# A written-out instruction order for local attention and a two-layer network: its first quarter ordered anew

## Chip, cores and metric

One core of one Trainium2 chip. The metric is the device time of one execution in microseconds (us), the median of the runs. In the text, PE is TensorE, DVE is VectorE, ACT is ScalarE, POOL is GpSimd and SP is SyncE, as the profile names them.

## What is computed

Attention with a window and a few global keys, then a two-layer network with a squared ReLU:

```python
# q, k, v: (4, 8, 768, 64) = batch, heads, sequence, head_dim; n_global 8, n_local 96
scores = scale * np.matmul(q, k.transpose(0, 1, 3, 2))
rel = pos[:, None] - pos[None, :]
is_global = pos[None, :] < n_global
is_local = (rel >= 0) & (rel < n_local)
dist = np.where(is_global & ~is_local, n_local, np.abs(rel))
scores = np.where(is_global | is_local, scores - slopes[:, None, None] * dist, -1e9)
a = softmax(scores)
x = (a @ v).transpose(0, 2, 1, 3).reshape(3072, 512)
h = np.maximum(x @ w_in, 0.0)      # w_in: 512 x 2048
return (h * h) @ w_out             # w_out: 2048 x 512
```

Inputs and output are float32; the kernel works in 16-bit floats with 32-bit sums.

## The kernel before

The 3072 tokens are cut into tiles of 128. Three tiles make a half, two halves a batch; there are eight halves, 0 to 7. Because of the window, a tile of queries needs the keys of its own tile ("own") and of the tile before ("before"); the global keys stand in the first 32 rows of a copy of the tile before (`kb` for keys, `vb` for values; "key fix" and "value copy" below).

For the first two halves (one batch) the work is listed job by job in `OPENING`. Its names are used throughout, with r for the tile, 0 to 5:

- T0, T1: TensorE transposes of q and k of tiles 0 and 1 (`turn_first`, L1233); Qr, Kr the same for a later tile (`turn_tile`, L1279).
- Pro, Prb: the distance term of the scores of tile r, own or before (`distances`, L1300). Sro, Srb: the scores (`score_tile`, L1314). ACT takes their exponent; for r from 3 on DVE multiplies by a mask (L1359).
- Ari: weights times values for two of the four head pairs, i = 0 or 1 (`attend_tile`, L1368); DVE normalises the result (L1392, L1394: "norm"). Xri: transposes of the normalised tile into `xt`, the input of layer 1 (`tile_to_x`, L1400).
- F, G, D, E: layer 1 (`layer1`, L705). Fc is four blocks of 128 hidden units for tile 0; Gci two blocks for tiles 1 and 2; Ec i and Dc the same for half 1. Later blocks of half 1 are single, with 384 columns.

From half 2 on, attention runs by head pair (`turn`, `score`, `attend`), and the two layers use sums of blocks, with seven products in place of eight. Those sums are DVE work.

The four weight loads of `w_in` (c0 to c3), the four of `w_out`, and all loads of q, k, v tiles except the first two tiles of q and k go through GpSimd's queue (L396, L454, L461). The queue is in order: a load that waits holds all behind it. The tiles `sq` and `sk` that loads of q and k write are one buffer each from half 2 on, so a load for half 3 waits until half 2's turns have read them. Half 1's q and k are staged in the memory that later holds `w_mix`, hence that name in the profile.

Nothing is scheduled while the program is built. `ORDER` is a list of words, and `Plan.run` calls the operations in that order; each engine executes its own in the order in which they were called and waits only for its data. A word is an engine's letter and a number: p is the n-th TensorE job in order of listing, l the n-th load, and a, d, g, s the n-th other operation, given to ACT, DVE, POOL or SP. What stands behind a dot names the PSUM banks (there are eight) that the job takes; behind a plus, the time to fill with idle matmuls; behind an @, an operation that the load follows. So the table fixes three things: the order on each engine, the engine of an operation that ACT or DVE could do, and the banks. A bank is free for the next job when the operation that reads it out has run.

Of the kernel before, what the change touches and what calls it, by code (L numbers as in the profile page):

```python
# [9 lines left out]
FP16 = mybir.dt.float16  # L10
# [3 lines left out]
P = 128  # L14
# [37 lines left out]
ORDER = """a4 d1 g2 p0.0 a6 s8 d12 a0 s10 d13 l3 l1 a18 l2 d15 d19 a26 d16 d3 l5 a30 d14 a20 a27 d9 l4 a23  # L52
d5 a22 d17 p1.12+31 a21 l0 p5.34 d11 a7 p10.56 l6 a28 p3 a24 l10 a31 d32 l9 a33 p6 d34 p4.7 a39
l7 p11 d37 a29 p9.0 p8.1 a46 l8 p2.23 d43 a40 p19.7 d35 l11 a47 p7 d55 a25 p13.51 d36 l13 a41
d44 p14.4 p12.67 d48 p15 a42 l12 d59 p17 a49 p16.0 p22.2 d45 l14 p24.4 a52 d51 p23.36 a50 d38
p34.50 l16 d58 a53 p21.7 d64 p25.2 a60 l18 p27.1 d65 a57 p20.4 a61 p32.37 d66 a81 d56 p31.2 l15
a73 p29.6 d68 p18.5 d72 p28.4 a74 p26.3 l19 p36.1 d54 a69 p35.2 p30.7 a86 d70 p33.54 d85 a71 d91
p39.16 a67 p40.27 a77 d63 p37.3 a82 d75 l17 a78 d62 p41.5 a92 d79 d76 p38.0 d84 d80 p45.4 d83
l21 a97 p48.1 d96 a101 l20 a98 p44.2 a89 p47.5 d107 l23 p46.7 a112 p42.0 d111 a108 d110 a93
p43.2 d109 p53.1 a87 p52.5 d102 p50.4 p49.7 a113 l22 d120 d100 a90 d105 p59.6 l27 a116 d119 a103  # L60
d106 p55.3 p51.1 l29 d94 a122 a88 d128 p65.2 l28 a104 d95 a117 p64.4 a118 p58.5 a129 a136 d114
p60.0 d99 a137 l30 d146 d191 p54.3 l24 p62.6 d115 d205 l25 p57.1 a133 p56.4 d125 d121 p63.7
p67.6 a123 d134 d135 a130 d206 p61.1 p72.3 a126 d132 p69.4 d189 a124 p77.7 a131 d156 p70.0 a142
p82.1 d157 d165 a159 p71.5 a160 p74.4 d162 l34 a166 d201 a163 p83.6 d147 a161 l26 p73.0 a167
d522 d164 a138 p84.3 l31 d158 d148 a168 a169 p79.52 d186 l35 a139 d202 p89.04 p81.1 d127 a198
l33 d151 p85 a187 d170 a178 d523 p86 a174 d207 a199 d184 p78.06 a179 d149 l32 p80.57 p88.41 d180
p87 a195 l36 d200 a175 p76.2 d203 a185 l37 d155 p75.4 a196 d193 p91.0 l38 a188 d143 s194 d197
p66.1 a181 l39 d172 a171 p95.3 d152 a173 p90.5 d223 p100.4 d153 a209 s224 a176 d236 p92 d204
p103.2 d177 d208 p68.3 d237 s216 a244 a140 d210 p93.6 d240 a211 p94 a182 d150 s217 a144 d219
p96.1 p104 d225 p97 d183 a245 d221 p98.7 s220 d239 a218 p102.3 d238 p111 d214 d228 s226 l44 p106  # L70
d222 d243 l43 d213 p109.61 s229 d227 p110.73 d154 p99 l40@217 a255 d258 s215 d141 p101 a256
l42@217 d145 a251 d272 d190 p113 l45 a252 a234 p114.73 d254 l41@217 d192 p108.61 p105.0 a248 l46
d246 a261 p107 d253 d259 a262 l47 d257 s260 p115.62 a249 s235 d230 p116.74 l48 p118.3 a264 d250
p131.1 a265 d232 d263 p117.6 a268 d231 a292 p122.2 d266 a273 p121.7 d233 a269 d212 p125.1 a271
d280 s324 p124 d284 p127.4 a283 p126 d241 a278 d267 p123.6 d285 a293 p137.1 s325 d281 p119.5
a287 p132 a286 p129.7 a279 d294 p130 p140 d323 a301 p142 d270 p134.6 a290 d274 a307 p128.1 a291
p135 d288 p133.2 a308 p136 d298 p141.5 a310 d300 s242 a299 p143.1 s282 a297 d309 p139 d326 p138
d524 p112 d395 l50@325 a305 s275 d311 p120 a303 l56 d306 a312 s289 d295 a302 p146.36 l53 p147.54
d304 p145.71 a330 s296 d313 l51@325 a333 p144.2 a331 d318 l52 p148.3 a334 d319 a276 l49@325
p149.5 d321 a327 a322 d433 d332 a328 l54 p151.64 p150.07 d314 p152 d320 a338 l57 d329 p159.1  # L80
a339 l55 p157.0 d336 a337 p172.7 a341 d340 p153 a352 d370 a342 p160.3 a350 d315 p169.6 s371 d353
a344 p158.7 p162 d351 p161 p154.4 d316 a355 d397 p166.3 a347 p164.7 d356 p163 s398 p156 d317
d358 d359 a366 p171.1 d343 p165 s399 p167 a360 d362 p181.7 a363 d335 a361 p170 d345 p175 d367
p177 a357 p174.0 d375 p173.5 a378 d373 p178.3 s247 s277 d369 p176 a383 s354 p180 d368 a372
p155.0 d349 a379 p168.1 a376 d382 a384 d400 p179 p183 l58@399 a364 p182.7 d380 a348 p184 s374
a377 l65 d385 p185.3 a389 l62 a387 d381 s386 p188.41 a365 d388 p187.05 l59@399 p186.27 a405
p189.6 d401 a409 l63 a413 d402 p190.0 a406 d416 l73 a410 d403 p191 a407 l61 d396 a414 p193.42
d412 a417 p194.65 l60@399 d411 a418 p192.71 p195 a422 d415 a419 l64 d391 p200.4 d429 a420 p206.7
d437 a426 p198.0 d392 p219.1 s438 d393 a434 d408 a427 p207.6 p204.4 d394 a447 s346 d489 p210
d443 a462 p202.5 a451 d428 p199.1 a423 d404 p211 a441 p213 d435 p197.4 p217.2 a432 d456 p205.5  # L90
s436 p218.1 d424 a444 d452 p196 d480 s491 a445 d476 a461 d460 p203.6 p215.7 d442 p223 a458 p221
d425 a453 p208 d421 s492 p209 d481 p220 a448 d483 p222.1 a469 d477 p214 a446 d467 p227.6 s390
d431 s468 p212.0 d457 p201 d449 a464 d493 a463 p216.1 d454 p224 a484 l70 p225 d459 s455 p230
a439 d473 a471 l66 d465 p226 a496 p231.50 d470 a474 l69@492 s430 p236.13 d478 p233.42 a497 s490
p228.7 d472 a503 l72 d482 a498 p229.5 l67@492 a509 d479 d494 a504 p241.4 l71 p235 a510 d485 d475
a527 d505 p237.01 a495 l68@492 a466 p232.72 d499 p234 l74 a500 d525 d486 a450 p245.3 d506 l75
p240.7 d508 p247 a512 s507 d515 p246.5 a533 p239 d488 a532 d487 d516 a526 p255 a501 p250 d520
p259.0 d544 s521 p249.2 d531 p243.6 d536 p252 a535 p238.3 d529 a540 d517 a513 p253 a549 d502
p261.5 s576 a519 p256 d514 p257.6 p270 d545 p263 d546 p244 a551 s440 a553 d541 a565 p248.1 d511
a530 p268.6 p272 d561 p267 a534 p251.2 d560 p260.4 a566 s562 p262 d537 p269 d550 p258.6 a542  # L100
p266 s547 d548 p242.4 a563 d538 a568 p254.0 a552 s577 d518 p264 a528 p271 a578 d554 p274 d567
d543 p265.7 p273 d579 p275 a580 a555 d569 p279 d558 a564 p281.2 d556 a596 a570 p276.60 a559 d585
s557 d571 p277.54 p278.71 a586 p280 d600 a593 s539 a589 d601 p282.6 a604 d603 a587 p286 a594
d598 d602 a590 p284.75 a605 d588 p283.03 p285.14 a609 p289 d595 a616 a613 s599 d668 p291 s574
a606 d619 d581 a607 p288.7 d572 p290.1 d622 a610 s575 d582 p303.0 a620 d591 p306.3 a639 d612
s573 p294 d608 a618 a643 d611 p323.5 a614 d671 d626 p305.4 p307 d642 p310 a644 p292.6 d584 d621
p295 a623 p321.4 d583 a628 d647 p296 d664 p312 d615 p298 s665 a629 p301 d650 p287.1 d632 p308.3
a617 s627 p297.4 d636 s597 p322 d645 p313.2 a666 d592 p299.6 a651 d631 p314 a648 p293.0 d652
p311.4 d624 p300 p316 d649 p315 a635 s625 p318.0 a633 d669 p302.4 d672 p309 a634 d655 p320 a667
p304 d653 p326 a662 d637 p324.2 d658 s638 a679 p325.7 a663 d646 s659 d640 p317 a678 p319 p335.4  # L110
# [94 lines left out]
def kernel(  # L205
# [11 lines left out]
    nc = tc.nc  # L217
# [1270 lines left out]
    for op in [*slope_ops, *mask_ops, *first]:  # L1488
        op.follows = [table_op]
# [117 lines left out]
```

## Time and profile before

| | us |
|---|---|
| median of 3 runs (lowest, highest) | 200.62 (200.59, 200.8) |
| the profiled execution | 200.43 |
| its span, first to last instruction | 198.7 |
| TensorE busy in the span | 191.6 |
| VectorE busy | 176.3 |
| ScalarE busy | 151.0 |
| GpSimd busy (nearly all of it issues loads) | 66.9 |

Rows of a view of groups or of the timeline give the start, the busy time, the engine, the line of the kernel and the operation with the tile that it writes and those that it reads. In square brackets is the idle time of the engine just before and what ended it. Rows of the waits give the total, the number and the longest. A load's row gives its size and the time from issue to landing.

### The profile page before, as it was taken

How to read it: one execution, taken by the hardware profiler on the slowest of the kernel's cores; microseconds unless marked ns; L12 is line 12 of the kernel's file. 1: busy time of each engine (PE TensorE's matmuls, PEld its weight loads, DVE VectorE, ACT ScalarE, POOL GpSimd, SP SyncE). 2: the span in 40 equal slices, each digit the busy share in tenths (PEclk: the TensorE clock that was granted, in tenths of full speed). 3: DMA queues.
4: the chain of work that ended last, by engine and by line, in shares of the span. 5: the costliest groups of instructions: out<-in, count | busy, mean ns of one | idle time of the engine just before them, and what ended most of it. 6: DMA issues, size and time to landing. Idle time of an engine off the chain costs nothing.

```text
span 198.7 us, 5980 instructions
## 1 busy us (share of the span) xinstructions
PE 191.6 (96%) x2381; PEld 163.2 (82%) x2381; DVE 176.3 (89%) x450; ACT 151.0 (76%) x321; POOL 66.9 (34%) x82
## 2 busy tenths in 40 slices
PE   7798999999999999999999999999999999999993
PEld 3576899856888687788888998999889999999993
DVE  7589696899999999999989999899899996978971
ACT  6799797899555888976999679878897578769211
POOL 8996565187108701940194007800000000000000
PEclk9999999999999999999999999999999999999999
DMA  5999999999999998999899799996531221201214
GB/s 152 182 150 194 189 180 172 209 195 155 182 192 92 155 205 218 107 127 145 218 118 153 104 222 129 161 175 147 102 102 37 94 57 40 109 0 53 109 53 158
DMA packets 106987, 27.52 MB, mean 139 GB/s; under 512 B 97104, under 2 KB 104016, under 8 KB 106960
## 3 DMA queue, kind: packets, MB, share of 16 engines
q0 software_dynamic: 74944, 13.11, 90.1%
q1 hardware_dynamic: 30816, 13.45, 31.7%
q10 hardware_dynamic: 1200, 0.59, 1.1%
q8 instruction: 18, 0.29, 0.6%
q14 instruction: 9, 0.07, 0.1%
HBM read 27.26 MB, written 6.29 MB: 169 GB/s over the span
## 4 chain that ended last, share of the span: by engine, by line
PE 78%; DMA 7%; POOL 5%; DVE 5%; ACT 3%; issue 1%; POOLq 0%; DVEq 0%
PE yps L1064 32%; PE hps L841 19%; PE hps L717 14%; PE sp L610 4%; DMA xt<-tm 4%; DMA w_mix<-in_k_dram 4%; PE av L671 3%; PE yps L978 3%; POOL w_mix L396 2%; POOL v L396 1%; DVE hr L901 1%; ACT h L758 1%; PE av L1380 1%; PE trp L549 1%; DVE vb L258 1%
## 5 line engine op out<-in xcount | busy, mean ns | idle before, releaser
L623 ACT ACTIVATE ex<-sp 128x512 f16<-128x512 f32 x66 | 36.7, 632 | 3.6 <-PE sp L610 3.5
L1064 PEld LDWEIGHTS <-h 128*128 128x128 f16 x376 | 33.9, 98 | 4.0
L717 PE MATMUL hps<-xt,w_in_sb 128*128 128x128 f16 (+2 forms) x288 | 35.6, 273 | 0.3 <-ACT ex L1350 0.3
L256 ACT COPY kept<-hps 128x384 f32<-128x384 f32 x52 | 24.6, 490 | 12.4 <-PE hps L841 8.8
L901 DVE CUSTOM_DVE_ANT_0 hr<-hps,kept 128x384 f16<-128x384 f32 x58 | 30.3, 548 | 1.0 <-PE hps L841 0.6
L717 PEld LDWEIGHTS <-w_in_sb 128*128 128x128 f16 x288 | 23.5, 98 | 5.9 <-DMA w_in_sb<-in_moe_w_in_dram 0.5
L1064 PEld LDWEIGHTS <-mixed 128*128 128x128 f16 x272 | 25.2, 98 | 3.6 <-DVE mixed L1029 0.2
L396 POOL DMA_DIRECT2D sq<-in_q_dram x19 | 17.3, 910 | 31.0 <-DMA q<-sq 23.4
L256 ACT COPY y<-yps 128x256 f32<-128x256 f32 (+2 forms) x39 | 14.6, 385 | 15.8 <-PE yps L1064 15.8
L396 POOL DMA_DIRECT2D sk<-in_k_dram x19 | 17.1, 903 | 24.9 <-DMA q<-sq 22.4
L841 PEld LDWEIGHTS <-w_in_sb 128*128 128x128 f16 x288 | 24.4, 98 | 1.0
L841 PEld LDWEIGHTS <-in_mix 128*128 128x128 f16 x272 | 22.8, 98 | 1.1 <-issue 0.3
L841 PE MATMUL hps<-x_mix,in_mix 128*128 128x192 f16 x204 | 23.4, 246 | 0.0
L1064 PE MATMUL yps<-w_mix,h 128*128 128x256 f16 (+1 forms) x192 | 22.4, 264 | 0.0
L1064 PE MATMUL yps<-w_mix,mixed 128*128 128x256 f16 (+1 forms) x184 | 22.2, 268 | 0.0
L396 POOL DMA_DIRECT2D v<-in_v_dram x24 | 21.8, 922 | 1.2 <-DVE h L760 0.6
L1064 PE MATMUL yps<-w_out_sb,h 128*128 128x256 f16 (+1 forms) x184 | 21.9, 268 | 0.0
L924 ACT ACTIVATE h<-hr 128x768 f16<-128x768 f16 x25 | 20.9, 857 | 0.0
L647 DVE TENSOR_TENSOR phat<-ex,mask 128x1024 f16<-128x1024 f16 (+1 forms) x36 | 20.6, 590 | 0.1
L744 ACT ACTIVATE hr<-hps 128x384 f16<-128x384 f32 (+1 forms) x35 | 18.5, 546 | 2.8 <-PE hps L717 2.8
L841 PE MATMUL hps<-xt,w_in_sb 128*128 128x192 f16 x172 | 19.8, 246 | 0.0
L1126 DVE TENSOR_TENSOR y<-yps,y 128x256 f32<-128x256 f32 (+1 forms) x30 | 11.9, 408 | 3.5 <-PE yps L1064 2.9
(110 smaller groups left out, 354.1 us busy)
## 6 DMA issues: line engine op xcount, KB each, us to landing
out_dram<-y SPq DMA_DIRECT2D x23, 256.0 KB, 2.6
v<-in_v_dram POOLq DMA_DIRECT2D x24, 128.0 KB, 7.1
sq<-in_q_dram POOLq DMA_DIRECT2D x19, 128.0 KB, 6.4
sk<-in_k_dram POOLq DMA_DIRECT2D x19, 128.0 KB, 6.4
w_in_sb<-in_moe_w_in_dram POOLq DMA_DIRECT2D x4, 512.0 KB, 11.0
w_out_sb<-in_moe_w_out_dram POOLq DMA_DIRECT2D x4, 512.0 KB, 12.3
y<-in_q_dram SPq DMA_DIRECT2D x2, 256.0 KB, 4.4
y<-in_k_dram ACTq DMA_DIRECT2D x2, 256.0 KB, 5.1
```

The source lines that it names most:

```text
L256: nc.scalar.copy(out=out, in_=in_)
L396: dma = nc.gpsimd.dma_start(out=dst, in_=src[x.b, :, r0 + t * P:r0 + (t + 1) * P, :] .rearrange("h p d -> p h d"))
L610: nc.tensor.matmul(sp[h][:, i, :], lhsT=lhsT, rhs=x.q[rows, r % HT, a, :], start=True, stop=True)
L623: nc.scalar.activation(out=st["ex"][:, h], in_=sp[h], func=AF.Exp, scale=scale)
L647: eng(e).tensor_tensor(out=x.phat[a][:, :, t0:t0 + n], op=ALU.mult, in0=st["ex"][:, :, i0:i0 + 2 * n].rearrange("p e (t b) c -> p e t (b c ...
L717: nc.tensor.matmul(st["ps"][:, i * n:(i + 1) * n], lhsT=w_in_sb[:, kk, m * P:(m + 1) * P], rhs=x.xt[:, kk, c0:c1], start=kk == 0, stop=kk ...
L744: nc.scalar.activation(out=o, in_=i, func=AF.Relu)
L841: nc.tensor.matmul(st[name][:, i * HC:(i + 1) * HC], lhsT=left(i, kk), rhs=right(kk), start=fresh and i == kk == 0, stop=kk == KK - 1, ski ...
L901: eng(e)._custom_dve(dve_ops.TENSOR_ADD_SAT, out=hidden(which)[:, :, cols], in0=sums(name), in1=st[kept], s0=3.4e38, s1=0.0)
L924: nc.scalar.activation(out=h2, in_=hr, func=AF.Square)
L1064: nc.tensor.matmul(st[bank_name][:, 0:n], lhsT=a(m), rhs=b(m)[:, cols], start=fresh and m == 0, stop=m == HK - 1, skip_group_check=not fresh)
L1126: eng(e).tensor_tensor(out=y, in0=ps, in1=y, op=ALU.add)
```

## The change

The table `ORDER` is new in its first part; the last 292 of the 383 TensorE jobs stand in the order that they had, as do the last 226 of ScalarE's operations, the last 294 of VectorE's and the last 45 of 76 loads, and all of SyncE's. The banks are renumbered all through. The first five TensorE jobs (the warm-up, T0, P0o, P1o, T1) and the first issues of the engines are the same.

```diff
 ORDER
-a4 d1 g2 p0.0 a6 s8 d12 a0 s10 d13 l3 l1 a18 l2 d15 d19 a26 d16 d3 l5 a30 d14 a20 a27 d9 l4 a23
+a4 d1 g2 s8 p0.0 a0 s10 l2 d12 d13 l3 a6 a18 l6 d3 a29 a22 d15 a30 d20 l4 d21 a24 a25 l5 a9 d5
...
-p43.2 d109 p53.1 a87 p52.5 d102 p50.4 p49.7 a113 l22 d120 d100 a90 d105 p59.6 l27 a116 d119 a103
-d106 p55.3 p51.1 l29 d94 a122 a88 d128 p65.2 l28 a104 d95 a117 p64.4 a118 p58.5 a129 a136 d114
+l30 d106 p46.1 a112 p43.6 d110 p52.2 p53.7 p45.5 a119 d105 a104 d99 p55.3 d100 p50.1 p59.2 d95
...
@@ score_tile, where its result tile is taken
-        st["ph", before] = phat_p.tile([P, 2, NPAIR, P], FP16, name="ph0", tag="ph0")
+
+        def weighted():
+            if ("ph", before) not in st:
+                st["ph", before] = phat_p.tile([P, 2, NPAIR, P], FP16, name="ph0", tag="ph0")
+            return st["ph", before]
...
-                nc.scalar.activation(out=st["ph" if added else "ex", before][:, h],
+                nc.scalar.activation(out=(weighted() if added else st["ex", before])[:, h],
...
-            eng(e).tensor_tensor(out=st["ph", before][:, :, a_], in0=st["ex", before][:, :, a_],
+            eng(e).tensor_tensor(out=weighted()[:, :, a_], in0=st["ex", before][:, :, a_],
...
@@ notes for the search that made the table; they emit nothing
+        slope_buf.used_by(st["job", before])
...
+    slope_buf = Buffer("ex", 4)
+    slope_buf.used_by(*slope_ops[1:])
```

In the second piece, p45 is G01, p46 A41, p43 A40, p52 and p53 X30 and X31, p50 X41, p55 X40, p49 and p59 G30 and G31; d106 is the value copy of tile 4, d110 and d105 are the norms of A41 and A40.

So the weighted tile of a score job is taken from its four buffers when it is first written, and no longer when the score job is listed.

The first place that the prediction speaks of is on VectorE, around the norms that the X jobs of half 1 need. `vb<-v` is a value copy (two rows: the copy and its global rows), `rec` and `tm` are the two instructions of a norm, `ph` is the product of exponents and mask, `xt<-trx` copies out an X job. Before, behind the value copy of tile 3:

```order
L258 COPY vb<-v 128x520
L258 COPY vb<-v 32x520
L1392 RECIPROCAL rec<-av 128x2x2
L1394 TENSOR_TENSOR tm<-av,rec 128x256
L1392 RECIPROCAL rec<-av 128x2x2
L1394 TENSOR_TENSOR tm<-av,rec 128x256
L1392 RECIPROCAL rec<-av 128x2x2
L1394 TENSOR_TENSOR tm<-av,rec 128x256
L760 TENSOR_TENSOR h_532<-hr 128x2x256 x2
L258 COPY xt<-trx 128x2x128
L1359 TENSOR_TENSOR ph_99<-ex,mask 128x2x256
L1392 RECIPROCAL rec<-av 128x2x2
```

Now, from the same copy:

```order
L258 COPY vb<-v 128x520
L258 COPY vb<-v 32x520
L1397 RECIPROCAL rec<-av 128x2x2
L1399 TENSOR_TENSOR tm<-av,rec 128x256
L1397 RECIPROCAL rec<-av 128x2x2
L1399 TENSOR_TENSOR tm<-av,rec 128x256
L258 COPY vb<-v 128x520
L258 COPY vb<-v 32x520
L1397 RECIPROCAL rec<-av 128x2x2
L1399 TENSOR_TENSOR tm<-av,rec 128x256
L1397 RECIPROCAL rec<-av 128x2x2
L1399 TENSOR_TENSOR tm<-av,rec 128x256
```

The norms are those of A30, A31, A41 and A40 in both. Tile 4's value copy has moved in between the second and the third, and the squares and products that stood ahead of the fourth have moved behind it.

The second place is on GpSimd, from the output weights on: the value loads (`v`) are half 2's, the loads of `sq` and `sk` half 3's. Before:

```order
L461 DMA w_out_sb<-in_moe_w_out_dram 128x4x512 x4
L396 DMA v<-in_v_dram 128x8x64 x2
L396 DMA sq<-in_q_dram 128x8x64
L396 DMA v<-in_v_dram 128x8x64
L396 DMA sk<-in_k_dram 128x8x64
```

Now:

```order
L461 DMA w_out_sb<-in_moe_w_out_dram 128x4x512 x4
L396 DMA sq<-in_q_dram 128x8x64
L396 DMA v<-in_v_dram 128x8x64 x3
L396 DMA sk<-in_k_dram 128x8x64
```

The load of q has moved ahead of all three value loads. The first two of these were those of tiles 0 and 1 of half 2, in this order; now tile 1's is the first and tile 0's the second. On VectorE, the value copy that reads both (L258, `vb<-v`) has the product for head pair 3 (L647, `phat`) directly behind it; before, that product stood ahead of it.

More of the change, by code (lines that the diff above doesn't have):

```diff
@@ L63 @@
[L63 to L74, printed above, removed]
@@ new lines @@
+l30 d106 p46.1 a112 p43.6 d110 p52.2 p53.7 p45.5 a119 d105 a104 d99 p55.3 d100 p50.1 p59.2 d95
+a116 a122 d94 a120 p57.6 a108 p54.1 d125 p51.3 a128 d121 a87 p63.7 p61.5 p58.6 a135 d132 a113
+d88 d129 a109 p83.2 d117 p62.1 d189 a118 p81.4 d187 a133 p56.5 a101 d102 p82.7 d123 p74.3 d126
+a124 p49.2 a186 a134 d188 p60.1 a114 p71.0 a130 p69.5 d162 a131 p77.6 d191 a127 p72.7 p64.2 d169
+a156 a174 d201 d163 p75.1 d165 d166 p76.3 d184 a167 a171 d164 p70.6 d157 p89.07 d202 l34 p88.41
+d203 a198 p65.5 d159 a195 d115 l25 d160 a172 p73.0 d158 a199 d161 l24 p84.4 d138 a168 d185 l26
@@ new lines @@
+a510 d505 a527 l75 d499 p237.52 a495 a466 p232.63 p234 d525 d486 a500 a450 p245.1 d506 p240.6
+d508 s507 p247 a512 d515 p246.7 a533 p239 d488 a532 d487 a526 d516 p255 a501 p250 d520 p259.5
+d544 s521 p249.3 d531 p243.0 p252 d536 a535 p238.1 d529 a540 s576 d517 a513 p253 a549 d502
+p261.7 a519 p256 a551 d514 p257.0 s440 p270 d545 p263 d546 p244 a553 d541 a565 p248.2 d511 a530
+p268.0 a534 p272 d561 a566 p267 p251.4 d560 s562 p260.3 a542 p262 d537 p269 d550 p258.0 s547
+a563 p266 d548 a568 p242.3 a552 d538 s577 p254.5 d518 a528 p264 a578 p271 d554 p274 d567 d543
@@ L123 @@
+a777 a778"""
 class Op:
```

111 lines of the change are left out of this document (56 added, 55 removed).

## The prediction

> **What bounds the kernel now.** I read the head of the page first, then the busy time by stretches, then the waits, then the loads. The page gives the span and the shares:
>
> ```profile
> span 198.7 us, 5980 instructions
> PE 191.6 (96%) x2381; PEld 163.2 (82%) x2381; DVE 176.3 (89%) x450; ACT 151.0 (76%) x321; POOL 66.9 (34%) x82
> ```
>
> TensorE (PE) has 7.1 us idle in 198.7. The busy time by stretches says where; I cut at 20.07, where layer 1 begins, and at 195.67, where TensorE has ended:
>
> ```profile
> core 0: us, PE busy (x) PEld busy (x) DVE busy (x) ACT busy (x) POOL busy (x), PEclk, DMA share, GB/s
> 0.00:20.07 20.07, 16.34 (x241) 11.46 (x242) 16.01 (x52) 16.54 (x38) 17.45 (x25) 1.00 1.79 170
> 20.07:60.00 39.93, 39.92 (x483) 32.76 (x484) 35.34 (x96) 31.59 (x67) 17.77 (x21) 1.00 1.78 184
> 60.00:100.00 40.00, 39.72 (x477) 31.64 (x476) 38.72 (x96) 31.81 (x69) 17.12 (x20) 1.00 1.72 158
> 100.00:195.67 95.67, 95.63 (x1185) 87.37 (x1182) 86.19 (x209) 70.85 (x151) 14.53 (x17) 1.00 0.72 105
> 195.67:198.70 3.03, 0.00 (x0) 0.00 (x0) 0.00 (x0) 0.27 (x1) 0.00 (x0) 1.00 0.39 130
> ```
>
> From 20.07 to 195.67 TensorE is idle for 0.01 + 0.28 + 0.04 = 0.33 us, at a granted clock of 1.00. The rest is 3.73 us ahead of 20.07 and 3.03 us of last copies and stores, which the change leaves alone. TensorE's waits, whole run:
>
> ```profile
> PE warm L324 <- DVE early L1466: 1.2, 1, 1.2
> PE sp L1330 <- ACT q L256: 0.9, 1, 0.9
> PE trp L1287 <- DMA w_mix<-in_k_dram: 0.7, 1, 0.7
> PE trp L1244 <- ACT sk L256: 0.4, 1, 0.4
> PE hps L717 <- ACT ex L1350: 0.3, 1, 0.3
> PE sp L1330 <- DVE tm L1394: 0.2, 1, 0.2
> ```
>
> The first is the kept start. The other five (0.9, 0.7, 0.4, 0.3, 0.2: 2.5 us) are what a better order of the opening could remove. Whether that is worth anything hangs on what starts layer 1. Here is the issue of its first weights (c1, the first of the two in the row), that load's time to landing, TensorE's first layer-1 weight load, and its first layer-1 matmuls:
>
> ```profile
> 11.46 1.55 POOL L454 DMA_DIRECT2D w_in_sb<-in_moe_w_in_dram  x2
> w_in_sb<-in_moe_w_in_dram POOLq DMA_DIRECT2D x1, 512.0 KB, 8.6
> 20.07 4.28 PEld L717 LDWEIGHTS <-w_in_sb 128*128 128x128 f16 x48 [0.47 <-DMA w_in_sb<-in_moe_w_in_dram]
> 20.07 4.56 PE L717 MATMUL hps<-xt,w_in_sb 128*128 128x128 f16 x48 [0.29 <-ACT ex L1350]
> ```
>
> 11.46 + 8.6 = 20.06: layer 1 starts as c1 lands. The list of waits names ACT for that 0.3; the weight-load queue, with 0.47 on the load, shows the real releaser. So the opening is paced by a load, and all that follows by TensorE's own work.
>
> **The change, part by part.**
>
> *The 39 jobs ahead of layer 1.* Both orders put the same 39 TensorE jobs first (warm-up, T, K, Q, P, S0 to S5, A0 to A2, X0 to X2). The eleven token loads ahead of c1 are reordered among themselves, c1 stays twelfth on GpSimd's queue, and no load ahead of it waits for a compute engine's result that comes late. So c1 lands at about 20.06 again, and removing the 2.5 us of waits before it is worth nothing. What has to hold is that the 39 jobs end by 20.06. The last token load (k of tile 4 now, of tile 5 before) keeps its slot, whose landing released TensorE at 17.60 in the old run:
>
> ```profile
> 17.60 0.62 PE L1287 MATMUL trp<-ident,w_mix 128*128 128x128 f16 x8 [0.69 <-DMA w_mix<-in_k_dram]
> 19.39 0.39 PE L1330 MATMUL sp<-q,kb 64*128 64x128 f16 x8
> ```
>
> With the job that it released, ten jobs were left, and they ended at 19.78 (19.39 + 0.39); now there are five: K4, S5 own, S4 own, S4 before, S5 before. K4's evacuation and key fix on VectorE stand between. I take the cover as enough, with some 0.5 us to spare; if it fails, each us past 20.06 is a us of the end. The three casts that swap engines and mask 4, which goes far back in ScalarE's order, lie under the same cover. Cost of all this: 0.
>
> *The new order from 20 to 27 us: term 1.* After G11, G10, F1, F0 the new order takes A30, A31, G00, A41, A40, X30, X31, G01 and then X40 (the diff's second piece). X40 needs A40's normalised tile. The rows of VectorE and then of TensorE that price this:
>
> ```profile
> 23.67 0.71 DVE L258 COPY vb<-v 128x520 f16<-128x520 f16 x2 [0.81 <-DMA v<-in_v_dram]
> 24.91 0.18 DVE L1392 RECIPROCAL rec<-av 128x4 f32<-128x4 f32 x1 [0.53 <-PE av L1380]
> 25.47 0.17 DVE L1392 RECIPROCAL rec<-av 128x4 f32<-128x4 f32 x1
> 28.52 0.63 DVE L258 COPY vb<-v 128x520 f16<-128x520 f16 x2
> 29.08 0.41 DVE L1359 TENSOR_TENSOR ph<-ex,mask 128x512 f16<-128x512 f16 x1
> 24.47 0.19 PE L1380 MATMUL av<-v,ph 128*128 128x65 f16 x1
> 26.09 0.19 PE L1380 MATMUL av<-v,ph 128*128 128x65 f16 x1
> 26.33 0.67 PE L1409 MATMUL trx<-ident,tm 128*128 128x128 f16 x6
> ```
>
> VectorE's copy for tile 3 starts at 23.67, as tile 3's values land; that load keeps its slot. Behind it the new VectorE order has norm A30, norm A31, the value copy of tile 4, norm A41, norm A40. A norm takes 25.47 - 24.91 = 0.56, a value copy 29.08 - 28.52 = 0.56: six steps, 23.67 + 6 x 0.56 = 27.03. TensorE gets to X40 sooner: F1 and four G take 24.47 - 20.07 = 4.40; three attends and F0 take 26.09 - 24.47 = 1.62; the fourth attend 26.33 - 26.09 = 0.24; X30 and X31 about 0.24 more. 20.07 + 6.50 = 26.57. Term 1 is 27.03 - 26.57, about **0.5 us**. In the old order two G pairs (G30, G31) stood between and covered it. Bounds: 0, if VectorE runs 0.5 ahead of this walk; 1.0, if one more norm stands in the way.
>
> *GpSimd's queue behind the output weights: term 2.* The load of q for half 3 (l34 of the table) was third behind the output weights, between the second and third value loads of half 2. It is now first, ahead of all three. It overwrites the staging tile that half 2's turns read, so it waits for the last turn. Here are GpSimd's rows at that place, the shortest landing time of such a load, three rows of VectorE, three pieces of the chain that ended last (TensorE's pace), and the first attend job of half 2:
>
> ```profile
> 39.42 0.88 POOL L396 DMA_DIRECT2D sq<-in_q_dram  x1 [4.04 <-PE trp L549]
> 40.28 0.88 POOL L396 DMA_DIRECT2D v<-in_v_dram  x1
> sq<-in_q_dram POOLq DMA_DIRECT2D x1, 128.0 KB, 6.4
> 47.64 0.61 DVE L258 COPY vb<-v 128x520 f16<-128x520 f16 x2 [0.24 <-DMA v<-in_v_dram]
> 49.11 0.67 DVE L647 TENSOR_TENSOR phat<-ex,mask 128x1024 f16<-128x1024 f16 x1
> 49.72 0.54 DVE L746 TENSOR_SCALAR hr<-hps 128x384 f16<-128x384 f32 x1
> 39.27 1.95 PE hps L717 x12
> 33.51 0.87 PE hps L717 x8
> 45.12 0.78 PE sp L610 x24
> 49.77 0.28 PE L671 MATMUL av<-v,phat 128*128 128x65 f16 x4
> ```
>
> The last turn also comes later: by then the new order has done five single 384-column blocks more (three take 1.95, so 0.65 each) and two 256-column pairs fewer (0.87 each): 3.25 - 1.74 = 1.51. With term 1 the waiting load starts at 39.42 + 1.51 + 0.5 = 41.43. An issue takes 40.28 - 39.42 = 0.86, so the two value loads behind it start at 42.29 (tile 1) and 43.15 (tile 0), and with 6.4 us to landing tile 0's values are there at 49.55. The copy that needs both started at 47.64 in the old run, on the second's landing; it moves by 1.9 us. In the new VectorE order the product for head pair 3 stands directly behind it (before, it was ahead): 49.55 + 0.56 + 0.61 (49.72 - 49.11) = 50.7. The attend job of pair 3 needs this product. TensorE was there at 49.77; the new order has one score unit less ahead of it (three take 0.78, so 0.26), and term 1 more: 50.0. Term 2 is 50.7 - 50.0, **0.7 us**. From below it is 0, if the landing came some 0.7 sooner; from above, with the old third value load's 9.0 us to landing in place of 6.4, it is 3.3:
>
> ```profile
> v<-in_v_dram POOLq DMA_DIRECT2D x1, 128.0 KB, 9.0
> ```
>
> The 9.0 was met with the output weights still in the queue; the new loads start 41.43 - 39.42 = 2.0 us later behind the same weights, so up to 2.0 of it is gone, and 9.0 - 2.0 = 7.0 is next to 6.4. I take 6.4, and so 0.7. The Trainium skill (DMA: Bandwidth & Descriptors, Anatomy of one DMA — SWDGE path) puts a transfer at about 2.0 us plus its bytes over 436 GB/s, an estimate of 2.3 us for 128 KB. By it the values would land at 45.5, term 2 would be 0 and the sum 0.5 (201.1); the rows here, 6.4 and more, speak against it.
>
> *Other parts.* Many operations change between VectorE and ScalarE; VectorE ends with four more (396 for 392). At 0.3 to 0.6 each, as its rows above, that is 1.2 to 2.4 us, and it is idle for 39.93 - 35.34 = 4.6 us of 20.07 to 60: 0. If it were full there, part of this would come on top of term 2. The late taking of the weight tile changes which of four buffers a tile gets, and no instruction: 0, since the attend jobs that read the old contents are several jobs back; else one attend, 0.24.
>
> **Sum.** Removed waits 0, term 1 0.5, term 2 0.7: +1.2 us. The profiled execution took 200.43 (its span of 198.7 and 1.73 around it), so 201.63. The median of the runs is 200.62, 0.19 above the profiled one: 201.8. A measurement of this kernel can tell about 0.2% (0.4 us) from no change.
>
> **The rivals.**
>
> *No wait survives.* The walk is some tenths too late in both places, VectorE and GpSimd keep ahead, and TensorE is as full as before: 200.6. For it: the old order has only 0.33 us of such waits in 175 us, so such an order can be met. Against: it needs both terms gone.
>
> *Faster: the opening's waits count.* If layer 1 could start when its 39 jobs are done, the 2.5 us would come off: 198.1. Against it: 20.06 is the load's landing to 0.01 us. What is left is c1 itself landing some 0.5 sooner, with fewer slow issues ahead of it: 200.1, since from there on the end follows one for one. A page bears on the cap. By the Trainium skill (Perfetto Trace Analysis, Identifying the Most-Contended Engine) matmul busy time does not show how near TensorE is to its limit, so a full row could hide time to win. The row of 48 holds 16 matmuls of 128 columns and 32 of 256, 10240 columns, in 4.40 us, 2.3 columns per ns; one of 384 columns takes 0.65/4 us, 2.4 per ns. The full stretch is full.
>
> *One wait alone.* Only term 1 or only term 2: 200.62 + 0.5 = 201.1 or 200.62 + 0.7 = 201.3.
>
> *VectorE stays behind.* The late copy shifts VectorE by 1.9 us and TensorE by 1.2. VectorE has little room to make good the difference (busy 38.72 of the 40 us from 60 on). If later attends or sums wait for it, up to 0.7 is added: 202.5. Against it: the old order kept TensorE full with VectorE that busy, so there is some lead between them.
>
> **Chances and range.** Both terms (201.8): 0.45. One alone: 0.20. VectorE behind (202.5): 0.08. No wait (200.6): 0.20. Faster by over 0.2%: 0.07. So slower 0.73, same 0.20, faster 0.07. Below 200.5 lie the faster cases and some of the even ones, about 0.12, and above 202.6 the long landings of term 2, about 0.05, so the range is 200.5 to 202.6. The likeliest case alone spans 201.3 to 202.4.
>
> **What would show it.** Right: the first weight load of layer 1 again at about 20.1 and again released by a load; a wait of TensorE on a norm near 27; GpSimd idle before the q load until about 41.4, the value copy at about 49.6 and a wait of TensorE on the head pair's product near 50. Wrong: layer 1 starting well before 20, or both places full and the end within 0.4 of the old one.

## The result, and the profile after

The kernel after takes 201.83 us (median of 5 runs, 201.37 to 202.39); the kernel before 200.62 (5 runs, 199.78 to 201.01). The ratio after to before is 1.0084, with a 95% interval of 1.006 to 1.0107: slower. The profiled execution took 202.39 us, the longest of the five, against 200.43 of before, so its trace shows about 2 us where the medians differ by 1.2. The profiled executions of two kernels below (the double edit, and the load ahead of c1) were disturbed; of these two only the times are used.

The head of the page, and the busy time in the same stretches as of before:

```profile
span 200.6 us, 5976 instructions
PE 191.7 (96%) x2381; PEld 162.9 (81%) x2381; DVE 178.9 (89%) x455; ACT 150.4 (75%) x316; POOL 66.6 (33%) x82
```

```profile
core 0: us, PE busy (x) PEld busy (x) DVE busy (x) ACT busy (x) POOL busy (x), PEclk, DMA share, GB/s
0.00:20.07 20.07, 15.75 (x241) 11.07 (x241) 16.23 (x54) 16.81 (x36) 17.07 (x25) 1.00 1.78 170
20.07:60.00 39.93, 38.66 (x461) 31.20 (x462) 36.09 (x93) 29.48 (x63) 17.88 (x21) 1.00 1.72 177
60.00:100.00 40.00, 39.72 (x474) 31.42 (x473) 38.53 (x97) 31.22 (x66) 16.21 (x19) 1.00 1.69 161
100.00:195.67 95.67, 95.67 (x1188) 87.56 (x1187) 87.39 (x212) 72.24 (x153) 15.44 (x18) 1.00 0.77 103
```

Behind the start of layer 1, all of TensorE's new idle time lies between 20.07 and 60: 39.93 - 38.66 = 1.27 us, where it was 0.01. (The opening has 16.34 - 15.75 = 0.59 us more as well; it lies ahead of c1's landing.) Its waits in that stretch:

```profile
PE av L671 <- DVE phat L647: 0.7, 1, 0.7
PE hps L717 <- ACT mask L337: 0.6, 1, 0.6
PE trx L1414 <- DVE tm L1399: 0.5, 1, 0.5
```

The 0.6 is the start of layer 1 (nearly all of it before 20.07); the other two are X40 and the first attend job of half 2, the two places of the prediction. Start of layer 1: the issue of c1 (first of the two), its time to landing, the last scores of the opening, the first weight load and the first matmuls.

```profile
11.20 1.55 POOL L454 DMA_DIRECT2D w_in_sb<-in_moe_w_in_dram  x2
w_in_sb<-in_moe_w_in_dram POOLq DMA_DIRECT2D x1, 512.0 KB, 8.9
18.89 0.68 PE L1331 MATMUL sp<-q,kb 64*128 64x128 f16 x16
20.12 0.44 PEld L717 LDWEIGHTS <-w_in_sb 128*128 128x128 f16 x5 [0.73 <-DMA w_in_sb<-in_moe_w_in_dram]
20.13 3.71 PE L717 MATMUL hps<-xt,w_in_sb 128*128 128x256 f16 x48 [0.56 <-ACT mask L337]
```

The opening ends at 18.89 + 0.68 = 19.57 and layer 1 starts at 20.13, as c1 lands (11.20 + 8.9 = 20.1). The list names ACT for the wait; the weight queue names the load.

The first place, VectorE's and TensorE's timelines:

```profile
25.38 0.86 DVE L258 COPY vb<-v 128x520 f16<-128x520 f16 x2
26.16 0.17 DVE L1397 RECIPROCAL rec<-av 128x4 f32<-128x4 f32 x1
26.91 0.42 DVE L1399 TENSOR_TENSOR tm<-av,rec 128x256 f16<-128x256 f32 x1
25.89 1.04 PE L717 MATMUL hps<-xt,w_in_sb 128*128 128x256 f16 x8
27.40 0.40 PE L1414 MATMUL trx<-ident,tm 128*128 128x128 f16 x4 [0.47 <-DVE tm L1399]
27.63 1.04 PE L717 MATMUL hps<-xt,w_in_sb 128*128 128x256 f16 x8
```

Norm A40 (26.91) ends the walk of six steps that began with tile 3's copy at 23.72. The view lists 0.47 us of idle, but the stall is more. The row of eight matmuls ahead of it is listed with 1.04 us, up to the end of the last one; where nothing stops the queue, the next job starts 0.87 us after such a row (28.50 - 27.63). So X40 could have come at 25.89 + 0.87 = 26.76 and is 0.64 late. The value copy of tile 4 is part of it: 26.16 - 25.38 = 0.78 us, where a value copy took 0.56 before. By themselves its two instructions, shortest, median and longest in ns:

```profile
L258 DVE COPY vb<-v x2: 285/412/540, 25.4 to 26.0; 128x520 f16<-128x520 f16 x1, 32x520 f16<-32x520 f16 x1
```

The second place, GpSimd, three of its loads one by one, VectorE, TensorE:

```profile
41.76 0.89 POOL L396 DMA_DIRECT2D sq<-in_q_dram  x1 [8.64 <-PE trp L549]
42.64 2.64 POOL L396 DMA_DIRECT2D v<-in_v_dram  x3
48.71 0.94 POOL L396 DMA_DIRECT2D sq<-in_q_dram  x1
49.58 2.70 POOL L396 DMA_DIRECT2D v<-in_v_dram  x3
sq<-in_q_dram POOLq DMA_DIRECT2D x1, 128.0 KB, 4.6
v<-in_v_dram POOLq DMA_DIRECT2D x1, 128.0 KB, 4.8
v<-in_v_dram POOLq DMA_DIRECT2D x2, 128.0 KB, 4.9
49.16 1.48 DVE L258 COPY vb<-v 128x520 f16<-128x520 f16 x2
50.57 0.67 DVE L647 TENSOR_TENSOR phat<-ex,mask 128x1024 f16<-128x1024 f16 x1
50.40 0.19 PE L671 MATMUL av<-v,phat 128*128 128x65 f16 x1
51.29 0.26 PE L671 MATMUL av<-v,phat 128*128 128x65 f16 x3 [0.70 <-DVE phat L647]
```

The q load waits until 41.76, the values land at 43.5 + 4.9 = 48.4, the copy starts at 49.16 and takes 50.57 - 49.16 = 1.41 us where it took 0.54 before, and the attend job stops after one matmul for 51.29 - 50.40 = 0.89 us (0.03 of it is that matmul's own). The copy has no wait in its bracket: the values had been there for some 0.8 us. VectorE itself was late; its busy time from the first turn's copy to that product (the stretch, its length, the time busy):

```profile
37.84:51.24 13.40, 13.33 (x35) 1.00 1.77 170
```

The same stretch of before:

```profile
37.75:49.78 12.03, 11.06 (x31) 1.00 1.81 181
```

From 37.8 on VectorE has almost no pause now (0.07 us), where it had 0.97; 0.87 us of its 13.33 is the slow copy itself. The job that follows both places in the two orders, 16 matmuls of layer 2, starts at 52.00, 1.92 later than in before (50.08); the last 40 matmuls of the run start at 194.78, 1.97 later (192.81). Nearly the whole loss is there by 52.

### The profile page after: what moved, and what is told of

The parts are those of the page before. It is cut to its first block, busy times and chain, and to the rows that moved or that the text cites. A ratio compares the mean times of both kernels' runs of the same rounds, so it can differ in the third digit from the quotient of the medians.

```text
span 200.6 us, 5976 instructions
## 1 busy us (share of the span) xinstructions
PE 191.7 (96%) x2381; PEld 162.9 (81%) x2381; DVE 178.9 (89%) x455; ACT 150.4 (75%) x316; POOL 66.6 (33%) x82
## 4 chain that ended last, share of the span: by engine, by line
PE 67%; DVE 13%; DMA 9%; POOL 6%; ACT 3%; issue 1%; POOLq 0%; DVEq 0%
PE yps L1064 31%; PE hps L841 19%; PE hps L717 8%; DMA v<-in_v_dram 5%; DMA xt<-tm 4%; PE sp L610 3%; PE av L671 3%; POOL w_mix L396 3%; DVE vb L258 2%; DVE hr L901 1%; POOL v L396 1%; DVE w_mix L488 1%; DVE hr L746 1%; DVE mixed L1029 1%; PE yps L978 1%
## 5 line engine op out<-in xcount | busy, mean ns | idle before, releaser
L717 PE MATMUL hps<-xt,w_in_sb 128*128 128x256 f16 (+2 forms) x288 | 35.4, 273 | 0.6 <-ACT mask L337 0.6
L256 ACT COPY y<-yps 128x256 f32<-128x256 f32 (+2 forms) x40 | 15.2, 391 | 16.9 <-PE yps L1064 14.2
L647 DVE TENSOR_TENSOR phat<-ex,mask 128x1024 f16<-128x1024 f16 (+1 forms) x36 | 20.7, 592 | 0.1
L744 ACT ACTIVATE hr<-hps 128x384 f16<-128x384 f32 (+1 forms) x32 | 16.7, 542 | 1.0 <-PE hps L717 0.9
L758 ACT ACTIVATE h<-hr 128x512 f16<-128x512 f16 (+1 forms) x20 | 14.4, 728 | 1.7 <-DVE hr L746 1.6
```

Source lines behind the costliest of these rows:

```text
L256: nc.scalar.copy(out=out, in_=in_)
L647: eng(e).tensor_tensor(out=x.phat[a][:, :, t0:t0 + n], op=ALU.mult, in0=st["ex"][:, :, i0:i0 + 2 * n].rearrange("p e (t b) c -> p e t (b c ...
L717: nc.tensor.matmul(st["ps"][:, i * n:(i + 1) * n], lhsT=w_in_sb[:, kk, m * P:(m + 1) * P], rhs=x.xt[:, kk, c0:c1], start=kk == 0, stop=kk ...
L744: nc.scalar.activation(out=o, in_=i, func=AF.Relu)
L758: nc.scalar.activation(out=h2, in_=hr, func=AF.Square)
```

## The experiments

Each time stands beside that of the kernel before, run alongside on the same chip; ratios are to that. "Head" is the start of that row of 16 matmuls, behind which TensorE has one order in all kernels, so it shows in one trace what each edit did ahead of it. The start of layer 1 differs by some tenths from trace to trace; the last column counts the head from it. An earlier start is partly lost again where a later load has not landed (see the copy on ScalarE), so neither column alone gives the worth of an edit.

| kernel | median us, before alongside | ratio, 95% interval | layer 1 starts | head | from layer 1 to head |
|---|---|---|---|---|---|
| before | | | 20.07 | 50.08 | 30.01 |
| after | 201.83, 200.62 | 1.0084, 1.006 to 1.0107 | 20.13 | 52.00 | 31.87 |
| values first | 201.42, 199.88 | 1.0071, 1.0043 to 1.0099 | 19.95 | 51.24 | 31.29 |
| X40 later | 201.41, 199.88 | 1.0078, 1.005 to 1.0107 | 19.74 | 51.58 | 31.84 |
| product first | 202.49, 199.88 | 1.0125, 1.009 to 1.0161 | 19.91 | 50.92 | 31.01 |
| X40 later, product first | 201.99, 199.88 | 1.0091, 1.0063 to 1.0119 | | | |
| before, q load first | 201.09, 200.11 | 1.0042, 1.0019 to 1.0064 | 20.06 | 50.08 | 30.02 |
| relu on ScalarE | 201.53, 200.11 | 1.006, 1.0034 to 1.0086 | 20.14 | 51.14 | 31.00 |
| copy on ScalarE | 201.41, 200.11 | 1.007, 1.0045 to 1.0095 | 19.82 | 51.47 | 31.65 |
| three repairs | 200.81, 200.11 | 1.0021, 0.9998 to 1.0044 | 19.98 | 50.48 | 30.50 |
| before, load ahead of c1 | 200.87, 199.98 | 1.0033, 1.0014 to 1.0052 | | | |
| matmuls before 20 | 201.97, 199.98 | 1.0107, 1.0066 to 1.0149 | 20.14 | 51.83 | 31.69 |
| matmuls after 20 | 202.49, 199.98 | 1.0112, 1.008 to 1.0145 | 19.83 | 51.94 | 32.11 |
| loads behind the copy | 201.56, 200.33 | 1.006, 1.003 to 1.009 | 20.45 | 51.20 | 30.75 |

**Values first.** The kernel after, with half 2's value loads ahead of the q load:

```diff
-l30 l34 l25 l24 l26 l31
+l30 l25 l24 l26 l34 l31
```

> The changed kernel, with half 2's three value loads put back ahead of the load of q for half 3 in GpSimd's queue; all else as it is. Theory of the prediction (the late landing of the values makes the second wait): the values land some microseconds sooner, TensorE's wait of about 0.9 us ahead of the first attend job of half 2 goes, and the time falls by about 0.7 us, to 201.1. Rival (VectorE's own queue is late there; in the changed kernel the values landed at 48.4 and VectorE came to the copy at 49.16): no gain, within 0.3 us of 201.8.

The wait at 50.4 is gone and the head comes 0.76 us sooner (0.58 counted from layer 1's start), but not because the values came sooner: VectorE reached the copy at 49.02, with no pause ahead of it as in after, and the copy took 0.79 instead of 1.41 us. The ratio falls by 0.0013, less than its interval, so the time does not part the two theories.

**X40 later.** The kernel after, with X40 behind G31:

```diff
-p55.3 p50.1 p59.2
+p50.1 p59.2 p55.3
```

> The changed kernel, with the transposes X40 moved behind the layer-1 pair G31 in TensorE's order; all else as it is. Theory (X40 waits for the norm of A40, which stands sixth behind tile 3's value copy): G31 covers the wait of 0.5 us near 27, and the time falls by 0.5 to 0.6 us, to 201.2. Rival (the loss sits elsewhere, or whatever is won here is waited for again at the attend job near 51, because VectorE is the late one there): 0 to 0.2 us.

X40 no longer waits, but the next job that needs VectorE does (A51, 0.28 us for its product), and the attend job of half 2 waits 0.69, where it waited 0.70. Counted from layer 1's start, the head comes 51.58 - 19.74 = 31.84 us later, as in after (31.87). An order that only moves TensorE's job back wins nothing where VectorE's row is what is late.

**Product first.** The kernel after, with the product of head pair 2 and one weight sum behind the product of pair 3 on VectorE:

```diff
-d151 d149 d148 d180 d205 d197 d206 d155 d200
+d151 d148 d180 d205 d206 d155 d200 d197 d149
```

> The changed kernel, with two operations of VectorE that nobody waits for yet (one weight sum, the product for head pair 2) moved behind the product for head pair 3: the value copy and that product come 1.2 us sooner in VectorE's order. Loads untouched. Rival (VectorE's queue makes the second wait): the wait of about 0.9 us goes and the time falls by 0.6 to 0.9 us, to about 201.1. Theory of the prediction (the values land too late): the copy waits for its load instead, and at most the 0.8 us between the landing at 48.4 and the copy at 49.16 can be won; with landings as late as predicted, nothing.

A miss, and the more telling for it. TensorE's longest wait after layer 1's start, its place, and the sum on VectorE that it is for:

```profile
PE yps L1064 <- DVE mixed L1029: 0.9, 1, 0.9
54.91 1.05 PE L1064 MATMUL yps<-w_mix,mixed 128*128 128x256 f16 x8 [0.92 <-DVE mixed L1029]
54.17 0.69 DVE L1029 TENSOR_TENSOR mixed<-h 128x1024 f16<-128x1024 f16 x1
```

The wait for the product is gone (head 50.92), and 0.92 us of another stands 4 us later, for a sum that VectorE reaches at 54.17, no sooner than in after (54.06): TensorE came 1.08 us sooner, VectorE did not. VectorE reached the value copy 1.29 us sooner (47.87), but the copy took longest here, 1.60 us to the product behind it. VectorE lacks time, not order. The double edit (both of the above in one kernel) agrees by its time.

> The changed kernel with both edits: X40 behind G31, and the two VectorE operations behind the product for head pair 3. If the two waits are the whole loss and add up: 1.2 to 1.5 us less than the changed kernel, the time of the kernel before (200.6 within 0.3). If VectorE stays behind further on, or the loss has another source (banks, engines of the moved operations): it keeps 0.5 us or more of it, 201.1 or above.

**Before, q load first.** One part of the change alone, in the kernel before:

```diff
-l30 l24 l25 l34 l26
+l30 l34 l24 l25 l26
```

> The kernel before, with one thing of the change: the q load of half 3 (l34) ahead of the first two value loads of half 2 on GpSimd's queue. Theory of the landing (as predicted): the values land 1.7 us later than in the kernel before plus up to 2.4 more, TensorE waits for the head pair's product near 50, and the kernel is 0.7 to 1.4 us slower than before (ratio 1.0035 to 1.007). Rival, VectorE's own queue: in the old order VectorE has 0.24 us of idle ahead of the copy and 0.6 us of lead on TensorE behind it; loads behind fewer output weights land in about 5 us, so the copy moves by 0.5 us or less and the time by 0 to 0.3 (ratio 1.000 to 1.0015).

The landing does cost in the old order, though not at the head pair's product near 50. GpSimd, the loads one by one, VectorE, TensorE:

```profile
39.40 0.88 POOL L396 DMA_DIRECT2D sq<-in_q_dram  x1 [6.50 <-PE trp L549]
40.28 2.62 POOL L396 DMA_DIRECT2D v<-in_v_dram  x3
sq<-in_q_dram POOLq DMA_DIRECT2D x1, 128.0 KB, 7.0
v<-in_v_dram POOLq DMA_DIRECT2D x1, 128.0 KB, 7.1
48.49 0.61 DVE L258 COPY vb<-v 128x520 f16<-128x520 f16 x2 [1.10 <-DMA v<-in_v_dram]
52.36 1.03 PE L1064 MATMUL yps<-w_mix,mixed 128*128 128x256 f16 x8 [0.37 <-ACT y L256]
53.66 1.05 PE L1064 MATMUL yps<-w_mix,mixed 128*128 128x256 f16 x8 [0.27 <-DVE mixed L1029]
```

The copy waits 1.10 us for its values and starts 0.85 later than in before (47.64); TensorE pays behind the head, at 52 and 53 (the layer-1 job behind the two waits starts at 54.55 for 53.69). The wait that names ScalarE is VectorE's too: ScalarE had waited 1.37 us for VectorE's relu, where it waited 0.51 before. And the landings stand at 46.4 (39.40 + 7.0) and 47.4 (40.28 + 7.1), to a tenth where they stand in after (41.76 + 4.6 and 42.64 + 4.8), though they are issued 2.36 us sooner. The kernel before has its own third load behind the output weights, the q load issued at 39.42:

```profile
sq<-in_q_dram POOLq DMA_DIRECT2D x1, 128.0 KB, 8.9
```

It lands at 48.3, and the third behind the weights lands at 48.4 here (41.15 + 7.3) and in after (43.5 + 4.9). So in these three kernels the hour of a landing goes by its place behind the weights and not by its issue: issued later, such a load lands no later. Moving q ahead moves both value loads back by one place, about 0.9 us.

**Relu on ScalarE.** The kernel after, with one relu of 512 columns given to the other engine:

```diff
-d138 a168
+a138 a168
```

> The kernel after, with one relu of 512 columns (0.60 us of VectorE at 43.48) given to ScalarE, which was idle for 0.92 us just behind that place. Theory of VectorE's queue: VectorE is full from 37.8 to 51.3, so the head pair's product comes 0.60 sooner, TensorE's wait of 0.70 near 50.4 falls to 0.1 to 0.3, and since VectorE is relieved and not only reordered nothing later takes it back: 0.5 to 0.6 us faster than after (ratio to before about 1.0055). Rival, what is won is waited for at the next place (as when the product alone was moved forward): the time of after within 0.2 us (ratio 1.0075 to 1.0085).

```profile
48.80 0.94 DVE L258 COPY vb<-v 128x520 f16<-128x520 f16 x2
49.67 0.67 DVE L647 TENSOR_TENSOR phat<-ex,mask 128x1024 f16<-128x1024 f16 x1
50.41 0.28 PE L671 MATMUL av<-v,phat 128*128 128x65 f16 x4
```

The two copies by themselves:

```profile
L258 DVE COPY vb<-v x2: 287/455/623, 48.8 to 49.1; 128x520 f16<-128x520 f16 x1, 32x520 f16<-32x520 f16 x1
```

The product starts 0.90 sooner than in after, the attend job does not wait, the head gains 0.86 and no other wait takes its place. Of the 0.90 only 0.36 is VectorE's earlier arrival at the copy (48.80 for 49.16); the other 0.54 is that the copy took 0.87 instead of 1.41, which the theory did not foresee. The ratio fits (1.006 for an expected 1.0055); alone it would not tell the theories apart, the trace does.

**Copy on ScalarE.** The kernel after, with the value copy of tile 4 on ScalarE:

```diff
-d106 p46.1 a112 p43.6 d110 p52.2 p53.7 p45.5 a119 d105 a104
+p46.1 a112 p43.6 d110 p52.2 p53.7 p45.5 a119 a106 d105 a104
```

> The kernel after, with the value copy of tile 4 (0.78 us of VectorE at 25.38, ahead of the norms that X40 waits for) given to ScalarE, which was idle from 26.9 to 27.8. Theory of the two waits: norm A40 is ready at 26.5, before TensorE gets to X40 at 26.76, the products that A51 waits for come sooner too, and 0.6 us comes off the end (ratio to before about 1.0055). Rival, later waits take it back: VectorE's full stretch begins when TensorE's turns release it at 37.8 and moves with them, so that would have to be a new wait between 28 and 37; then the time of after within 0.2 us.

```profile
23.83 0.19 PE L1385 MATMUL av<-v,ph 128*128 128x65 f16 x1 [0.30 <-DMA v<-in_v_dram]
26.88 0.40 PE L1414 MATMUL trx<-ident,tm 128*128 128x128 f16 x4
```

X40 does not wait. In this execution layer 1 began 0.31 us sooner than in after (19.82), and the attend job behind its first blocks then waited 0.30 for its values and started at 23.83, just as in after: that landing is the next limit, and it caps what an earlier c1 could win. So of X40's 0.64 the head gains 0.53, though counted from layer 1's start it is 0.22. The ratio (1.007) lies between the two expectations and its interval holds both; the place is shown by the trace.

**Three repairs.** The relu, the copy and the values first together.

> The kernel after, with the relu of the second run and the copy of the third on ScalarE, and the three value loads of half 2 ahead of the q load as in an earlier run. If the two waits are all that the change costs: 0.6 + 0.6 + 0.3 = 1.5 us off, and the kernel is within 0.3 us of before (ratio 0.999 to 1.0015). If something else in the new order costs as well (more switches between kinds of TensorE jobs, later waits): 0.5 us or more stays (ratio 1.0025 and above).

```profile
20.07:60.00 39.93, 39.86 (x480) 32.55 (x480) 35.96 (x93) 31.95 (x66) 17.85 (x21) 1.00 1.78 184
```

The row has the columns of the table of stretches above. TensorE is full again, the head comes at 50.48, and the ratio of 1.0021 (0.9998 to 1.0044) has its whole interval below after's. The two places are where most of the cost is; what is left (0.40 us at the head, 0.49 counted from layer 1's start) no run settles, and the rival's 0.5 us lies within the interval.

**Loads behind the copy.** The kernel after, with GpSimd held until half 2's value copy has run (the copy's function returns its instruction for that):

```diff
-l36 d206 a170 d155
+d206 a170 d155 l36@155
```

> The kernel after, with one wait more on GpSimd: the q load that was issued at 48.71, and the value loads queued behind it, wait for half 2's value copy on VectorE, so that GpSimd issues nothing beside that copy. Theory that the copy is slow because GpSimd issues loads beside it: its two instructions take 0.54 us as in the kernel before, not 1.41, the head pair's product is ready at about 50.3, TensorE (there at 50.40) hardly waits, and 0.6 to 0.9 us comes off the end (ratio to before about 1.004 to 1.0055) unless the loads, now 1.0 us later, are waited for further on. Rival, the copy is slow for another reason (the half's length, landing data): it takes 1.2 us or more again, TensorE waits 0.5 to 0.7 us near 50.4, and the time is that of after within 0.2 us (ratio 1.0075 to 1.0095).

VectorE's two copies by themselves, then the rows at that place:

```profile
L258 DVE COPY vb<-v x2: 284/288/292, 49.2 to 49.5; 128x520 f16<-128x520 f16 x1, 32x520 f16<-32x520 f16 x1
50.13 0.88 POOL L396 DMA_DIRECT2D sq<-in_q_dram  x1 [1.29 <-DVE vb L258]
49.76 0.67 DVE L647 TENSOR_TENSOR phat<-ex,mask 128x1024 f16<-128x1024 f16 x1
50.47 0.28 PE L671 MATMUL av<-v,phat 128*128 128x65 f16 x4
```

The same two in after:

```profile
L258 DVE COPY vb<-v x2: 614/724/834, 49.2 to 49.8; 128x520 f16<-128x520 f16 x1, 32x520 f16<-32x520 f16 x1
```

VectorE gets there at the same time (49.22 for 49.16), the copies take 0.28 each instead of 0.61 and 0.83, the product starts 0.81 sooner, and TensorE does not wait. The loads that were held back cost nothing visible ahead of 60. The ratio (1.006, 1.003 to 1.009) lies between the two expectations and does not part them; the trace does. So the second place is the copy held up by GpSimd's issues, on a VectorE with no time to spare for it.

**The start of layer 1.** Three kernels. The kernel before with one more load of 128 KB ahead of c1:

```diff
+            if c == 1:
+                nc.gpsimd.dma_start(out=spare, in_=v[0, :, 0:P, :].rearrange("h p d -> p h d"))
```

> The kernel before, with one more load of 128 KB (a tile of values into memory that is free there) on GpSimd's queue directly ahead of c1. Theory that c1's landing starts layer 1: c1 is issued 0.87 us later (one issue), lands 0.8 to 1.3 us later, layer 1 starts at 20.9 to 21.4, and the end follows one for one: 0.8 to 1.3 us slower than before (ratio 1.004 to 1.0065). Rival, the opening's jobs start layer 1 (they end at 19.78 in the kernel before): layer 1 starts within 0.3 us of 20.07 and the time stays within 0.3 us.

And the kernel after with 0.65 us of idle matmuls ahead of the last scores of the opening, or inside layer 1:

```diff
-p39.56
+p39.56+65
```

```diff
-p41.0
+p41.0+65
```

> The kernel after, with three matmuls of 512 columns on zeros (0.65 us of TensorE, results unused) ahead of S5 own, so before layer 1. Theory that c1's landing starts layer 1: the 39 jobs, which ended at 19.57, now end near 20.2, layer 1 starts within 0.15 us of its time, and the time is that of after within 0.2 us (ratio to before 1.0075 to 1.0095). Rival, the opening's jobs count: 0.5 to 0.65 us slower than after (ratio 1.011 or more).

> The kernel after, with the same three matmuls ahead of G10, so inside layer 1. Theory that TensorE is the bound from 20 on: 0.65 us slower than after where no wait takes it up (ratio 1.0115). Rival, the waits on VectorE near 27 and 50 set the pace: VectorE has the 0.65 us to catch up, the wait at 27 goes (0.64 of stall), and the time is that of after within 0.2 us (ratio 1.0075 to 1.0095).

The later c1 costs 0.0033 (0.0014 to 0.0052), some 0.7 us for one issue of 0.87. That fits a landing that carries through to the end, somewhat below the expected 0.8; the start of layer 1 was not seen here, and the rival's 0.3 us lies at the lower bound of the interval.

With the matmuls ahead of 20 layer 1 starts at 20.14 (20.13 in after), as the theory said, but not for its reason. The first weight load and the first matmuls:

```profile
19.96 0.93 PEld L717 LDWEIGHTS <-w_in_sb 128*128 128x128 f16 x8 [0.23 <-DMA w_in_sb<-in_moe_w_in_dram]
20.14 3.72 PE L717 MATMUL hps<-xt,w_in_sb 128*128 128x256 f16 x48 [0.23 <-ACT ex L1355]
```

c1 had landed by 19.96. What the matmuls waited for is ScalarE's exponent of scores that now came later: it ended at 20.09 (19.49 + 0.60), where it ended at 19.68 in after. So 0.65 us used up the opening's cover and about 0.2 us more; that the two starts agree is luck. The head even comes 0.17 sooner than in after. The times of these two kernels are too wide to part the theories (1.0107 and 1.0112, both intervals hold 1.0084).

Inside layer 1 the matmuls leave 0.24 of their 0.65 us at the head, counted from layer 1's start: between the two expectations, nearer to the rival. X40's wait falls from 0.47 to 0.22, as the value copy of tile 4 takes 0.54 us there instead of 0.78.

## Why the prediction was right, and where it was not

**The sum** was 1.2 us, the medians differ by 1.21; the ratio puts it at 1.2 to 2.1 us, with 1.7 in the middle. That the sum and the medians agree to 0.01 us is luck: each of the two terms was a little small, and one has another cause than the one that was reckoned. In the trace the way from layer 1's start to the head is 31.87 instead of 30.01, 1.86 more, of which the two stalls are 0.64 + 0.86 = 1.50. The remaining 0.36 is of the size of what the three repairs leave (0.40 to 0.49), and is open.

**Removed waits, 0:** right, by the landing of c1 at 20.1 and the weight load that waited for it; the load ahead of c1 fits. (The agreement of 20.06 with 20.07 in the prediction is closer than a landing time given to 0.1 us can bear.) The cover of 0.5 us was thinner than it looked. TensorE's jobs ended 0.56 us ahead of c1, but the exponent that layer 1 also waits for ended only some 0.4 us ahead of it. With the matmuls before 20 it was used up, and in the kernel with the loads behind the copy the opening waited 0.8 us elsewhere and layer 1 began at 20.45, with the weights already there.

**Term 1, 0.5:** right in place and mechanism. TensorE at 26.76 (predicted 26.57), the norm at 27.25 (27.03); the second value copy took 0.78 instead of 0.56. Listed 0.47, in effect 0.64. That slower copy is 0.22 of the 0.64 and was not foreseen: its first instruction took 0.54 us beside an issue of GpSimd (up to 25.83), 0.28 in the kernel with the matmuls after 20, where X40's wait is 0.25 less. What the step didn't say either is that it is a lag of VectorE and not of one norm: moved away from X40, it is paid at A51.

**Term 2, 0.7:** right in place and nearly in size (0.70 listed, 0.86 in effect), wrong in cause, so that its size is luck. The waiting load started at 41.76 (predicted 41.43). The step that failed is "with 6.4 us to landing tile 0's values are there at 49.55": they were there at 48.4, as the time to landing shrank with the later issue. The 6.4 was taken for a floor; 4.9 lies below it. Taking the 2.0 us of later issue from the old 9.0 was the right rule on the wrong load: the 9.0 is that of the fourth load behind the weights, which landed at 49.3 (40.28 + 9.0), and tile 0's values are now the third. The third landed at 48.3 in the kernel before, and that hour, carried over, would have been right. The Trainium skill's fit (DMA: Bandwidth & Descriptors, Anatomy of one DMA — SWDGE path), 2.3 us by its estimate for 128 KB, is no match for these queued loads either: 7.0 and 4.6 us for the same load.

What stood in its place is the line "Other parts ... 0", with the 4.6 us of VectorE's idle time from 20 to 60 as cover. That idle time was there, 3.8 us after, but not where it was needed: only 0.07 us of it lay between 37.84 and 51.24. Copies of the turns that ScalarE had made were now VectorE's (four of k in that stretch instead of one), and the value copy, pushed to 49.16, met GpSimd's issues and took 0.87 more. 49.16 + 0.56 + 0.61 = 50.33 would have been in time for TensorE at 50.40, and was in the kernel with the loads behind the copy. The prediction's own condition ("If it were full there") was the case.

**The rivals.** No wait, and faster, did not come. "VectorE stays behind" was right as a cause and wrong as an addition: no third wait follows in after, but any edit that only reorders (X40 later, product first) meets it. The landing that the prediction relied on is real in the old order (q load first: 1.10 us of wait); in the new one VectorE came later still and hid it.

## What to carry to other kernels

Idle time of an engine covers added work only where it lies: cut the busy view at the wait that is meant to be covered, not at the stage. Behind the output weights a load's landing went by its place in the queue here, so carry over the hour of landing of that place, not the duration, when an issue moves. An instruction that takes longer than the same one elsewhere may be held by another engine: look at what runs beside it. And where two engines are full, tell a late order from a lack of time by moving the suspected work to a third engine; moving it along the same one only shows where the wait goes next.

## What the runs showed of the hardware

- A value copy of 2 instructions takes 0.58 us by itself and up to 1.64 beside loads that GpSimd issues: 0.28 and 0.29 with GpSimd held, 0.61 and 0.83 in after, 0.81 and 0.83 with the product first. In after the first ends at 49.78 and the second at 50.64, each 0.1 to 0.2 behind the end of an issue (49.65, and about 50.5 for the first of the three from 49.58 on). The Trainium skill (SBUF — State Buffer, Who interferes with whom) has VectorE's fast copies and GpSimd share one pair of ports under an exclusive lock, and the later one wait for the whole instruction; that fits these rows. It doesn't explain why the copies of the q load first, beside an issue from 48.75 on, took 0.28 and 0.30. Nor is a copy held by every issue that it starts in: with the relu on ScalarE the first copy began 0.12 us into an issue (48.80, the issue from 48.68 to 49.63) and took 0.29, and only the second, begun at 49.1, was held to 0.62; in after the first began 0.45 us into one and was held. Which part of an issue holds a copy is open.
- The wait that a view lists is shorter than the stall, by 0.17 and 0.16 us at the two places. Both are what the last row before the wait is listed with beyond the time to the next job: 1.04 - 0.87 = 0.17 for eight matmuls of layer 1, 0.19 - 0.03 = 0.16 for one of the attend job.
- Executions of one kernel differ by more than a per mille: five of the kernel before lie between 199.78 and 201.01. The stretch behind the head, where TensorE's order is the same, shows it too. In the trace of before the last 40 matmuls start 142.73 us after the head, with the three repairs 142.36, with the values first 142.02, with the matmuls after 20 143.83: waits of 0.2 us near 86 to 89 come and go, and the last of these has one of 0.56 at 108.7. Edits of 0.3 us can't be told by these times, only by the trace ahead of the head.
